# Retention and a GELU feed-forward: three stores on another queue, two loads on another queue, and k ahead of v in one chunk

## The chip, the cores and the metric

The kernel runs on one core of a Trainium2 chip. The metric is the device time of one execution in microseconds (us); the time given is the median of several runs. Five engines work side by side, each with its own instruction stream: TensorE (PE, matrix products), VectorE (DVE), ScalarE (ACT), GpSimd (POOL) and SyncE (SP). SP only issues transfers here; ACT and POOL issue transfers between their other instructions. An instruction that waits holds up everything behind it on its own engine.

## The reference

Four batches, eight heads, a sequence of 768 and a head size of 64. For every head, a decaying state is updated and read at each step:

```
state = gamma[None, :, None, None] * state + einsum('bhd,bhe->bhde', k[:, :, t], v[:, :, t])
y[:, :, t] = scale * einsum('bhd,bhde->bhe', q[:, :, t], state)
```

The result, as 3072 tokens of 512 numbers, goes through a feed-forward of width 2048:

```
h = x @ w_in
g = 0.5 * h * (1.0 + tanh(c * (h + 0.044715 * h * h * h)))
return g @ w_out
```

Inputs and output are 32-bit floats; the kernel multiplies in 16 bits.

## The kernel before

The sequence is cut into six chunks of 128 steps. A chunk has four batches, so (c,b) names the work of chunk c and batch b. For each (c,b) q, k and v are loaded (256 KB each, `load1`, L101 to L105), scaled by the decay and cast to 16 bits (`prep1`, L176 to L194), and for chunks 0 and 1 q and k are transposed on PE (`mm_T`, L235; T(c,b) in this text). From there follow the scores (`mm_A`, L260), masked on DVE (L278), the output y (`mm_yc`, `mm_yi`), and the new state (`mm_s`, `ev_S`). Then comes the feed-forward of the chunk: `moe1` or `moe1_two` (h and GELU, 16 blocks of 128) and `moe2` (the second product), whose result `ev_O` (L458 to L466) copies from PSUM to `o_sb` and stores to memory.

The order of every engine is written out by hand: instructions run on each engine in the order in which the program lists them. `run(units, after)` (L484) goes through a list of pieces of PE work and puts other work after the piece with a given number.

Around the change:

- While PE does the second product of chunk 0, chunk 1 is prepared. `preps(1, b)` (L586) scales q on DVE, scales k on POOL and casts v on ACT. The stores of chunk 0 are issued by POOL, between these k scalings.
- Chunk 1 is loaded by SP (L591 to L599), except v(1,0) and v(1,1), which ACT issues between its GELUs (L577). `hold` (L126) makes the first of SP's loads wait until part of w_out has landed.
- `load(2)` (L615) puts all loads of chunk 2 on SP. q comes in 16 pieces of 64 KB, in a layout that DVE can transpose (`load_blk`, L107); k and v come batch by batch, v first. From chunk 3 on, k is also loaded in 16 such pieces, beside its ordinary load.
- For chunk 2 POOL does all preparation: for each batch it scales q, scales k, casts v (`prep`, L207). PE still transposes k of chunk 2.
- q is kept in two buffers, k and v in six buffers each; `o_sb` has four.

Of the kernel before, what the change touches and what calls it, by code (L numbers as in the profile page):

```python
# [16 lines left out]
def kernel(  # L17
# [9 lines left out]
    nc = tc.nc  # L27
    B, H, S, Dh = q.shape
    C = 128
    NCk = S // C  # L30
# [49 lines left out]
    BLK = {"q": (2, 3, 4, 5), "k": (3, 4, 5)}  # L80
# [12 lines left out]
    def ld_tile(nm, c, b):  # L93
        if nm == "q":
            t = ld_all(("q32", c)).rearrange("p (b hp) a d -> p b (hp a d)", b=B)
            return t[:, b].rearrange("p (h d) -> p h d", h=H)
        if (nm, c, b) not in raw:
            raw[nm, c, b] = ld.tile([128, H, Dh], F32, tag=f"{nm}32", bufs=6, name=f"{nm}32")
        return raw[nm, c, b]

    def load1(eng, nm, c, b):  # L101
        eng.dma_start(  # L102
            out=ld_tile(nm, c, b),
            in_=srcs[nm][b, :, c * C:(c + 1) * C, :].rearrange("h p d -> p h d"),
        )  # L105

    def load_blk(nm, c):  # L107
        t = ld_all((nm + ("32" if nm == "q" else "T32"), c))
        src = srcs[nm].rearrange("b (hp j) s (dd d) -> j dd s (b hp) d", j=2, dd=2)
        for j in range(2):  # L110
            for dd in range(2):
                for a in range(4):
                    p0, t0 = (2 * j + dd) * 32, c * C + a * 32
                    nc.sync.dma_start(  # L114
                        out=t[p0:p0 + 32, :, a, :], in_=src[j, dd, t0:t0 + 32]
                    )

    def load(c):
        for nm in "qk":
            if c in BLK[nm]:  # L120
                load_blk(nm, c)
        for b in range(B):
            for nm in "vk":
                load1(nc.sync, nm, c, b)

    def hold(nm, c, b, until):  # L126
# [19 lines left out]
        out=misc[:, 0:1], in_=zero[:, 0:1], func=AF.Gelu_apprx_tanh, scale=1.0  # L146
# [16 lines left out]
    for j in range(2):  # L163
        for hp in range(NHP):
            nc.vector.tensor_scalar(
                out=mask[:, j, hp],
# [291 lines left out]
    def ev_O(c, b):  # L458
        ps = o_ps[c, b]
        rows = out[b * S + c * C:b * S + (c + 1) * C, :]  # L460
        o_sb = op.tile([128, d_model], F32, tag="o", name="o_sb")
        if b == B - 1 and c > 0:
            nc.vector.tensor_copy(out=o_sb, in_=ps)
        else:
            nc.scalar.copy(out=o_sb, in_=ps)  # L465
        (nc.scalar if c == NCk - 1 else nc.gpsimd).dma_start(out=rows, in_=o_sb)  # L466

    def moe2_last(c, b):

# [20 lines left out]
    VE, AC, PO, SY = nc.vector, nc.scalar, nc.gpsimd, nc.sync  # L490
# [88 lines left out]
    def units2(c, b, n=4, tag="o"):  # L579
        u = [(lambda i=i: moe2(c, b, range(i, i + n), tag)) for i in range(0, NF, n)]  # L580
        last = u[-1]
        u[-1] = lambda: (last(), ev_O(c, b))
        return u
# [10 lines left out]
    load1(SY, "k", 1, 1)  # L594
    load1(SY, "q", 1, 2)
    load1(SY, "k", 1, 2)
    load1(SY, "v", 1, 2)
    for nm in "qkv":
        load1(SY, nm, 1, 3)  # L599
    u = [units2(0, b, tag="ooho"[b]) for b in range(B)]  # L600
    run(
        [u[i % 3][i // 3] for i in range(12)] + u[3],
# [10 lines left out]


    load(2)  # L615
    for b in range(B):
        prep(2, b)
# [9 lines left out]
            4: [(att_AY, 1, (3,), "o", 1, (), VE)],  # L627
            6: [(att_S, 1, 3)],
            8: [(att_T, 2, 0), (load, 3)],
            10: [(att_T, 2, 1)],  # L630
            12: [(att_AY, 1, (), "o", 2, (0, 1), None)],
# [17 lines left out]
    for c in range(2, NCk - 1):  # L649
        n = c + 1  # L650
        after = {
            2: [(prep, n, 0)],
            4: [(prep, n, 1)],
            6: [(prep, n, 2), (att_T, n, 0)],
            8: [(prep, n, 3), (att_T, n, 1)],
            9: [(load, n + 1)] if n + 1 < NCk else [],
            12: [(att_AY, n, (), "att", n, (0, 1), None)],
            13: [(att_T, n, 2)],
            15: [(att_T, n, 3)],
            18: [(att_AY, n, (0, 1), "h", n, (2, 3), VE)],  # L660
            20: [(att_S, n, 0)],
            21: [(att_S, n, 1)],
            25: [(att_AY, n, (2, 3), "h", n, (), AC)],
            27: [(att_S, n, 2)],
            28: [(att_S, n, 3)],
        }
        run(
            [(lambda fc=fc: moe1(c, fc)) for fc in range(NF)]
            + [x for b in range(B) for x in units2(c, b)],
            after,  # L670
        )
    c = NCk - 1
# [36 lines left out]
```

## Time and profile before

| what | value |
|---|---|
| median of 9 runs | 219.75 us (219.18 to 220.63) |
| the profiled execution | 219.52 us |
| its span in the trace | 217.4 us |
| TensorE's granted clock | 1.0 in all of the span |
| transfers | 32.88 MB, mean 151 GB/s |
| POOL's stores, L466 | 20, 256 KB each, median 3.4 us to landing |
| SP's loads of k and of v, 256 KB each | 22 and 20, median 4.6 us to landing |
| SP's loads of q in pieces of 64 KB | 64, median 2.7 us to landing |

The profile is one execution. Its page has the busy time of each engine; the span in 40 slices (5.4 us each) with the busy share in tenths; the transfers by queue; and the costliest groups of instructions, by source line. A row of the timeline has the start, the duration, the engine (SPq and ACTq are the transfers that an engine issues; their duration is that of issuing), the line, the operation, what is written and read, and in brackets the idle time just before it with the engine that ended it. The time to landing runs from the start of the issue until the data has arrived.

### The profile page before, as it was taken

Reading aid. Unit: us, or ns where it says so; the run is one execution under the profiler, and the core shown is the slowest. Engines: PE = TensorE matmul, PEld = TensorE weight load, DVE = VectorE, ACT = ScalarE, POOL = GpSimd, SP = SyncE. Lnnn points to the kernel's source line nnn. Section 1 sums busy time; section 2 is a strip of 40 time slices with the busy share of each in tenths; the row PEclk is TensorE's granted clock in tenths of the full one; section 3 lists DMA queues with packets and bytes.
Section 4 is the critical chain, followed back from the end, with each engine's and each line's share of the span. In section 5 each row is a group of like instructions: output and inputs, shape, how many; then the busy total and the mean of one; then the engine's idle time right before and its main releaser. Section 6 shows DMA issues by size and latency. Waiting matters only on the chain.

```text
span 217.4 us, 3916 instructions
## 1 busy us (share of the span) xinstructions
PE 207.7 (96%) x1544; PEld 113.0 (52%) x1544; DVE 85.5 (39%) x152; ACT 87.3 (40%) x150; POOL 98.9 (46%) x119
## 2 busy tenths in 40 slices
PE   7889999969999999999999999999999999999993
PEld 2447644426877655444555444545444545444462
DVE  3445200198844671333781343691253650100001
ACT  2575563134454333266314165213276223466120
POOL 3699200271449722599613699511399411000000
PEclk9999999999999999999999999999999999999999
DMA  7999999997989778997589986488920011200112
GB/s 173 288 248 207 207 204 239 207 303 138 189 184 204 115 147 175 256 263 124 87 155 226 275 169 95 63 161 197 269 87 3 0 48 62 86 0 0 51 64 81
DMA packets 124225, 32.88 MB, mean 151 GB/s; under 512 B 118064, under 2 KB 122544, under 8 KB 124208
## 3 DMA queue, kind: packets, MB, share of 16 engines
q1 hardware_dynamic: 109632, 20.32, 48.0%
q0 software_dynamic: 5824, 9.44, 17.6%
q10 hardware_dynamic: 8752, 2.88, 5.4%
q8 instruction: 12, 0.20, 0.3%
q14 instruction: 5, 0.04, 0.1%
HBM read 30.53 MB, written 6.29 MB: 169 GB/s over the span
## 4 chain that ended last, share of the span: by engine, by line
PE 85%; SPq 5%; DMA 3%; ACT 2%; POOL 2%; issue 1%; DVE 1%
PE o_ps L445 37%; PE h_ps L412 34%; SPq L114 5%; PE spin_ps L152 4%; DMA k<-in_k_dram 3%; PE a_ps L265 3%; PE y_ps L300 3%; PE s_ps L319 2%; PE y_ps L287 2%; PE qkT_ps L242 1%; POOL k L188 1%; ACT qkT L224 1%; ACT g L427 1%; SPq L102 0%; POOL q L199 0%
## 5 line engine op out<-in xcount | busy, mean ns | idle before, releaser
L445 PE MATMUL o_ps<-w_out,g 128*128 128x512 f16 (+1 forms) x400 | 88.1, 371 | 0.0
L412 PE MATMUL h_ps<-xT,w_in 128*128 128x512 f16 (+2 forms) x488 | 86.6, 334 | 0.5 <-ACT g L427 0.5
L427 ACT ACTIVATE g<-h_ps 128x512 f16<-128x512 f32 (+1 forms) x98 | 57.4, 588 | 50.7 <-PE h_ps L412 50.7
L412 PEld LDWEIGHTS <-w_in 128*128 128x128 f16 x488 | 45.7, 98 | 36.9 <-issue 0.7
L445 PEld LDWEIGHTS <-g 128*128 128x128 f16 x400 | 37.7, 98 | 38.8
L278 DVE TENSOR_TENSOR a_sb<-a_ps,mask 128x512 f16<-128x512 f32 x48 | 30.1, 682 | 19.7 <-PE a_ps L265 19.7
L466 POOL DMA_DIRECT2D out_dram<-o_sb x20 | 11.4, 568 | 49.0 <-ACT o_sb L465 39.4
L188 POOL TENSOR_TENSOR k<-k,cst 128x512 f16<-128x512 f32 x24 | 25.5, 1062 | 15.1 <-DMA k<-in_k_dram 15.1
L465 ACT COPY o_sb<-o_ps 128x512 f32<-128x512 f32 x19 | 11.1, 586 | 47.2 <-PE o_ps L445 42.0
L345 POOL TENSOR_TENSOR stg<-st,cst 128x512 f32<-128x512 f16 x16 | 16.4, 1044 | 12.8 <-DVE st L336 11.7
L336 DVE TENSOR_TENSOR st<-s_ps,stg 64x256 f16<-64x256 f32 x32 | 13.5, 421 | 17.8 <-PE s_ps L319 17.2
L199 POOL TENSOR_TENSOR q<-q,cst 128x512 f16<-128x512 f32 x16 | 16.7, 1042 | 1.9 <-DMA q<-in_q_dram 1.9
L251 DVE STREAM_TRANSPOSE qkT<-q 128x512 f16<-128x512 f16 x16 | 11.2, 699 | 12.1 <-POOL q L199 12.1
L188 DVE TENSOR_TENSOR q<-q,cst 128x512 f16<-128x512 f32 x7 | 7.6, 1090 | 18.5 <-DMA q<-in_q_dram 18.5
L224 ACT CAST xT<-y_ps 128x512 f16<-128x512 f32 x15 | 8.3, 588 | 14.9 <-PE y_ps L300 14.8
L199 POOL TENSOR_TENSOR kT<-kT,cst 128x512 f16<-128x512 f32 x12 | 12.5, 1042 | 0.0
L152 PE MATMUL spin_ps<-zero 128*128 128x512 f16 x32 | 10.6, 477 | 1.2 <-DVE zero L144 1.2
L478 DVE COPY o_sb<-o_ps 128x256 f32<-128x256 f32 x1 | 0.4, 425 | 25.2 <-PE o_ps L445 25.2
L185 POOL CAST v<-v 128x512 f16<-128x512 f32 x16 | 9.6, 601 | 0.0
L226 DVE CAST xT<-y_ps 128x512 f16<-128x512 f32 x9 | 5.9, 686 | 7.8 <-PE y_ps L300 7.8
L251 DVE STREAM_TRANSPOSE qkT<-kT 128x512 f16<-128x512 f16 x12 | 8.3, 689 | 1.8 <-POOL kT L199 1.8
L300 PE MATMUL y_ps<-a_sb,v 128*64 128x128 f16 x192 | 8.6, 223 | 0.2 <-DVE a_sb L278 0.2
(33 smaller groups left out, 93.5 us busy)
## 6 DMA issues: line engine op xcount, KB each, us to landing
k<-in_k_dram SPq DMA_DIRECT2D x22, 256.0 KB, 4.6
v<-in_v_dram SPq DMA_DIRECT2D x20, 256.0 KB, 4.6
out_dram<-o_sb POOLq DMA_DIRECT2D x20, 256.0 KB, 3.4
q<-in_q_dram SPq DMA_DIRECT2D x64, 64.0 KB, 2.7
kT<-in_k_dram SPq DMA_DIRECT2D x48, 64.0 KB, 2.7
w_in<-in_moe_w_in_dram POOLq DMA_DIRECT2D x4, 512.0 KB, 9.3
w_out<-in_moe_w_out_dram POOLq DMA_DIRECT2D x4, 512.0 KB, 14.7
q<-in_q_dram SPq DMA_DIRECT2D x6, 256.0 KB, 5.2
```

Of the source, the lines that this page charges most:

```text
L152: nc.tensor.matmul(out=ps, lhsT=zero[:, 0:128], rhs=zero, start=True, stop=True)
L188: eng.tensor_tensor(out=t, in0=src, in1=cst[:, col:col + H].unsqueeze(2).broadcast_to([128, H, Dh]), op=ALU.mult,)
L199: nc.gpsimd.tensor_tensor(out=t, in0=ld_all((key, c))[:, b * NHP:(b + 1) * NHP].rearrange("p hp a d -> p (hp a) d"), in1=cst[:, col:col + ...
L251: nc.vector.transpose(out=t[:, i].rearrange("p hp t -> p (hp t)"), in_=blk16.pop((nm, c, b)).rearrange("p ha d -> p (ha d)"),)
L278: nc.vector.tensor_tensor(out=s, in0=ps[j], in1=mask[:, j], op=ALU.mult)
L300: nc.tensor.matmul(out=y_ps[j * 64:(j + 1) * 64, hp], lhsT=h16["v", c, b][:, 2 * hp + j], rhs=a_sb[c, b, j][:, hp], start=(c == 0), stop=True,
L336: eng.tensor_tensor(out=st[sl, :, b, sl], in0=s_ps[sl, :, sl], in1=stg[sl, :, b, sl], op=ALU.add,)
L345: nc.gpsimd.tensor_tensor(out=stg[:, :, b], in0=st[:, :, b], in1=cst[:, OG:OG + NHP].unsqueeze(2).broadcast_to([128, NHP, 128]), op=ALU.mult,)
L412: nc.tensor.matmul(out=out, lhsT=w_in_sb[wi][:, kc, wr * 128:(wr + 1) * 128], rhs=xT[c][:, kc, t0:t1], start=(kc == 0), stop=(kc == NHP - ...
L427: nc.scalar.activation(out=out, in_=in_, func=AF.Gelu_apprx_tanh, scale=1.0)
L445: nc.tensor.matmul(out=ps[:, n0:n1], lhsT=g_sb[c, fc // 2][:, fc % 2, b * C:(b + 1) * C], rhs=w_out_sb[fc // (NF // NO)][:, fc % (NF // NO ...
L466: (nc.scalar if c == NCk - 1 else nc.gpsimd).dma_start(out=rows, in_=o_sb)
```

## The change

Three edits. The stores of chunk 0 are issued by SP for batches 0, 1 and 2, and by POOL only for batch 3. v(1,2) and v(1,3) are issued by ACT, behind its last GELU of chunk 0, so that SP issues eight loads of chunk 1 and not ten. And in chunk 2, the only one that `load` fills without a block load of k, the order of each batch's loads is k, v.

```diff
         for b in range(B):
-            for nm in "vk":
+            for nm in "vk" if c in BLK["k"] else "kv":
                 load1(nc.sync, nm, c, b)
...
-        (nc.scalar if c == NCk - 1 else nc.gpsimd).dma_start(out=rows, in_=o_sb)
+        if c == NCk - 1:
+            eng = nc.scalar
+        else:
+            eng = nc.sync if c == 0 and b < B - 1 else nc.gpsimd
+        eng.dma_start(out=rows, in_=o_sb)
...
     load1(SY, "k", 1, 2)
-    load1(SY, "v", 1, 2)
-    for nm in "qkv":
-        load1(SY, nm, 1, 3)
+    load1(SY, "q", 1, 3)
+    load1(SY, "k", 1, 3)
+    load1(AC, "v", 1, 2)
+    load1(AC, "v", 1, 3)
```

On SP the order is now: q and k of chunk 1, the three stores, the 16 pieces of q of chunk 2, then k and v of chunk 2.

## The prediction

> **What bounds the kernel now.** I read the page first: the totals, then the slices.
>
> ```profile
> PE 207.7 (96%) x1544; PEld 113.0 (52%) x1544; DVE 85.5 (39%) x152; ACT 87.3 (40%) x150; POOL 98.9 (46%) x119
> ...
> PE   7889999969999999999999999999999999999993
> ...
> DMA  7999999997989778997589986488920011200112
> ```
>
> TensorE (PE) is busy for 207.7 of 217.4 us, and the granted clock is full in every slice. A change that takes no matmul away can only win PE's holes. After the start they lie in slice 9 (a 6, at 43 to 49 us) and around 65 us; from 73 us to the end nothing is listed as waited for by PE. The DMA engines are nearly full up to 60 us. So next come PE's waits in 33 to 73 us, and the rows of its timeline that carry them ("[2.08 <- ...]" is the idle time before the row and who ended it).
>
> ```profile
> PE qkT_ps L242 <- DVE q L188: 2.1, 1, 2.1
> PE qkT_ps L242 <- POOL k L188: 0.6, 2, 0.4
> ```
> ```profile
> 47.73 0.40 PE L242 MATMUL qkT_ps<-iden,q 128*128 128x128 f16 x4 [2.08 <-DVE q L188]
> ...
> 64.72 0.40 PE L242 MATMUL qkT_ps<-iden,k 128*128 128x128 f16 x4 [0.23 <-POOL k L188]
> ...
> 67.28 0.40 PE L242 MATMUL qkT_ps<-iden,k 128*128 128x128 f16 x4 [0.42 <-POOL k L188]
> ```
>
> The three holes, 2.08 + 0.23 + 0.42 = 2.73 us, are the stake. The first is transpose T(1,1) (chunk 1, batch 1), which waits for q(1,1) scaled on VectorE (DVE). Its row and GpSimd's (POOL's) rows beside it:
>
> ```profile
> 44.14 3.53 DVE L188 TENSOR_TENSOR q<-q,cst 128x512 f16<-128x512 f32 x1
> ```
> ```profile
> 43.04 0.63 POOL L466 DMA_DIRECT2D out_dram<-o_sb  x1 [2.33 <-ACT o_sb L465]
> 43.90 0.56 POOL L466 DMA_DIRECT2D out_dram<-o_sb  x1 [0.23 <-ACT o_sb L465]
> 44.48 1.05 POOL L188 TENSOR_TENSOR k<-k,cst 128x512 f16<-128x512 f32 x1
> 45.46 0.58 POOL L466 DMA_DIRECT2D out_dram<-o_sb  x1
> 46.06 1.05 POOL L188 TENSOR_TENSOR k<-k,cst 128x512 f16<-128x512 f32 x1
> ```
>
> The same q row takes 0.68 or 0.69 at 38.80, 49.39 and 52.40. Here it takes 3.53 and ends at 47.67, 0.56 after POOL's unbroken run from 43.90 to 47.11. I read it as DVE held while POOL works without a gap, then running its 0.69.
>
> The other two holes are chunk 2's k, from the DMA by way of POOL:
>
> ```profile
> 59.60 1.05 POOL L199 TENSOR_TENSOR q<-q,cst 128x512 f16<-128x512 f32 x1 [1.85 <-DMA q<-in_q_dram]
> 63.62 1.04 POOL L188 TENSOR_TENSOR k<-k,cst 128x512 f16<-128x512 f32 x1 [2.97 <-DMA k<-in_k_dram]
> 64.61 0.61 POOL L185 CAST v<-v 128x512 f16<-128x512 f32 x1
> 65.19 1.04 POOL L199 TENSOR_TENSOR q<-q,cst 128x512 f16<-128x512 f32 x1
> 66.19 1.03 POOL L188 TENSOR_TENSOR k<-k,cst 128x512 f16<-128x512 f32 x1
> ```
> ```profile
> 45.61 11.27 SPq L114 DMA_DIRECT2D q<-in_q_dram  x16
> 56.98 0.47 SPq L102 DMA_DIRECT2D v<-in_v_dram  x1
> 57.49 0.94 SPq L102 DMA_DIRECT2D k<-in_k_dram  x1
> ```
>
> v(2,0) is issued at 56.98 and lands 3.2 later, at 60.2; k(2,0) lands 6.1 after its issue, at 63.6. That is 1.8 more than the second load of chunk 3 (4.2) or chunk 4 (4.4).
>
> **Part 1: three stores leave POOL for SyncE (SP).** POOL loses three issues: 0.63 + 0.56 + 0.58 = 1.77 us. More important, k(1,1) no longer stands behind two stores that wait for ScalarE's (ACT's) copies. k(1,1) landed at 42.2 and k(1,2) at 44.0 (issue plus latency), so POOL can scale k(1,1) from 42.3 and be idle when DVE comes to q(1,1) at 44.14; q(1,1) landed at 40.5. DVE then ends at 44.9, before PE reaches T(1,1) at 45.65. Gain 2.08, if POOL is idle at 44.14. If both k scalings stood in the way back to back (2 x 1.05, from 44.1), DVE would end at 46.9 and the gain be 0.8; later k landings (part 2) move POOL's k(1,2) away, so I take 2.08. What is late next is chunk 2's k.
>
> A row of the trace bears on this twice: beside POOL's k rows at 7.71 and 10.42, which grew from 1.04 to 1.31, DVE's q rows (7.43, 10.14) kept 0.69; whoever came second waited. The Trainium skill, "GPSIMD Engine Reference", section "8. Key points", says that GpSimd shares its SBUF interfaces with VectorE, and that instructions with two SBUF inputs contend; the q scaling is one, so these rows agree. By the rule alone, which names no DMA issue, the k scalings still collide and up to 1.3 of the 2.08 would stay; the sum above goes by the rows.
>
> On SP the stores stand behind k(1,3) and ahead of all of chunk 2's loads. The third can't be issued before ACT's copy, 44.33 + 0.58 = 44.91. A 256 KB store from SP isn't in this trace. From below: ACT's own stores, 0.34 to 0.36 an issue. From above: SP's loads issued from 37.8 to 44.3, up to 1.32. So the 16 q pieces start between 45.3 and 48.2 (k(1,3) issued until 44.3, then 3 x 1.3), against 45.61. They took 11.27 for 16; the shortest are 0.49 + 0.05, so 8.6. Their end (now 56.88) moves by d between 45.3 + 8.6 = 53.9 (d = -3.0) and 48.2 + 11.27 = 59.5 (d = +2.6). In the compiled list of instructions and their waits each load reuses one of eight completion counters, and the eighth q piece waits until the third store has landed: issue near 45.7 plus the 5.1 of the store at 45.46 now gives 50.8, against 51.56 now; eight more pieces keep their 0.53 to 0.6. I take d = -0.8.
>
> **Part 2: v(1,2), v(1,3) on ACT.** Two issues leave SP (1.32 + 1.23); the same bytes move through the same, already full DMA engines, so the chunk's last load lands about when it did (50.0). In the compiled list ACT's issue of v(1,2) waits on the counter that q(1,1) used, so ACT stands from 34.12 until about 40.5; behind it stand v(1,0)'s cast and the copies of o_sb. Cover: ACT did nothing between 34.12 and 42.16 but that cast (0.62). Issues cost 0.38 each (as at 27.48 and 29.21) to 1.67 (at 3.03): ACT is free at 40.5 + 0.8 + 0.6 = 41.9, or 44.5 at worst. PE needs the bank of the first o_ps again at 44.61, and its copy takes 0.58: loss between 0 and 0.5. I take 0, the nearer rows. The two v loads share with k(1,1), q(1,2), k(1,2): k(1,2) may land up to 2 x 0.9 (the spacing from 42.2 over 43.1 to 44.0) later than 44.0, at 45.8; with everything 2.08 earlier, T(1,2) is due at 49.0, and POOL's 1.05 still fits.
>
> "DMA: Bandwidth & Descriptors", section "Issuing engines are not separate DMA queues", of the Trainium skill says that another issuing engine saves only sequencer time; no row here shows the move, and by the rule alone part 2 would be worth 0.
>
> **Part 3: k before v in chunk 2.** No instruction is added; k(2,0) takes the first place, which lands at 60.2 + d. POOL scales it right after q(2,0), so one k scaling (1.03) goes from in front of v(2,0)'s landing. Cover for the later v: s and y matmuls need it only after 76 us.
>
> **The sum.** PE without waits would reach T(2,0) at 64.72 - 0.23 - 2.08 = 62.41, and T(2,1) at 67.28 - 2.73 = 64.55. POOL's k(2,0) is ready at 59.6 + d + 1.04 + 1.04 = 61.7 + d: no hole. For k(2,1) it depends on the second load.
> *A. The second load is 1.8 late again.* v(2,0) lands at 63.56 + d; then cast, q, k: T(2,1) at 67.28 - 1.03 + d = 66.25 + d = 65.45, a hole of 0.9. Gain 1.03 - d = 1.83: 219.52 - 1.83 = **217.7**.
> *B. It isn't late.* POOL runs without a gap, k(2,1) is ready at 64.4 + d. Gain 2.73: 216.8.
> After that POOL's chain ends k(2,3) 1.0 + |d| earlier than now, still ahead of T(2,3). From 73 us on PE waits for nothing, and chunk 3's k loads land by about 97.5 against uses up to 105, so the gain is kept.
>
> The profiled execution took 219.52 (span 217.4 and 2.1 around it); the median of the nine is 219.75, 0.23 above, so the median may come out 0.2 higher than the sum.
>
> **Rivals.**
> *C. DMA gives less:* A with d between 0 and +0.8, since stores queue in front of the q pieces. For: full DMA engines up to 50 us. Against: nothing is added to the bytes. Gain 0.2 to 1.0, near 218.8.
> *Nothing:* d near +1.0 in A, the hole merely moves from 47 to 67 us: 219.5. Or the change doesn't do what it says: v(1,2) goes out not behind the GELUs but 6 us later, so part 2 is idle; A and B don't rest on it.
> *Slower:* one mechanism: SP, in order, stands at the three stores, and chunk 2's loads start late. It decides from d = +1.03, q pieces issued until 57.9; at the bound d = +2.6 it costs 1.6: 221.1. For: the third store can't go before 44.91, and SP was never idle there. Against: the store takes the place of a load that SP issued in just that time.
>
> **How the numbers follow.** A 0.45, B 0.25, C 0.12, nothing 0.08, slower 0.10. A measurement of this kernel tells about 0.2% (0.4 us) from no change. Faster is A + B + C = 0.82. The range reaches from B (216.8, less 0.2 for its unknowns) over A and nearly all of C to 219.0.
>
> **What would show it.** Right: DVE's q(1,1) at 0.7; no PE hole near 45.7; the last q piece issued by 56; PE's k hole at T(2,1) 0.9 (A) or none (B). Wrong: q(1,1) still over 1.5; SP's q pieces starting after 47; ACT's first o_sb copy after 43.5; a hole at T(2,0); new holes beyond 73 us.

## The result and the profile after

The changed kernel takes 216.97 us (median of 16 runs, 216.50 to 218.05); the kernel before, on the same chip, takes 219.51 (median of 53). The ratio is 0.9902 with a 95% interval of 0.9883 to 0.9921, so it is about 2.15 us faster (219.51 x 0.0098). The profiled execution took 217.77, with a span of 215.5; it is one of the longer ones.

The page of the changed kernel, the same three rows as before:

```profile
PE 207.4 (96%) x1544; PEld 112.9 (52%) x1544; DVE 82.8 (38%) x152; ACT 87.1 (40%) x150; POOL 96.7 (45%) x116
...
PE   7989999999989999999999999999999999999993
...
DMA  7999999997899787998779976589910012100111
```

PE's busy time is the same within 0.3 us; the 6 of slice 9 has become a 9. What is left of the holes is an 8 in slice 12 (59 to 65 us).

PE's waits of the changed kernel in 33 to 75 us, and the transposes that carried them before, from PE's timeline:

```profile
PE qkT_ps L242 <- POOL k L188: 1.4, 2, 1.0
```
```profile
45.21 0.39 PE L242 MATMUL qkT_ps<-iden,q 128*128 128x128 f16 x4
...
62.79 0.40 PE L242 MATMUL qkT_ps<-iden,k 128*128 128x128 f16 x4 [0.98 <-POOL k L188]
...
65.35 0.40 PE L242 MATMUL qkT_ps<-iden,k 128*128 128x128 f16 x4 [0.42 <-POOL k L188]
```

T(1,1) at 45.21 has no bracket: it waits for nothing. T(2,0) waits 0.98 where it waited 0.23, T(2,1) 0.42 as before.

DVE's row of q(1,1), and POOL's rows around it and in chunk 2:

```profile
43.87 0.68 DVE L188 TENSOR_TENSOR q<-q,cst 128x512 f16<-128x512 f32 x1
```
```profile
41.83 1.04 POOL L188 TENSOR_TENSOR k<-k,cst 128x512 f16<-128x512 f32 x1 [1.22 <-DMA k<-in_k_dram]
45.23 1.04 POOL L188 TENSOR_TENSOR k<-k,cst 128x512 f16<-128x512 f32 x1 [2.36 <-DMA k<-in_k_dram]
...
60.68 1.05 POOL L199 TENSOR_TENSOR q<-q,cst 128x512 f16<-128x512 f32 x1 [5.61 <-DMA v<-in_v_dram]
61.69 1.04 POOL L188 TENSOR_TENSOR k<-k,cst 128x512 f16<-128x512 f32 x1
```

q(1,1) takes 0.68 instead of 3.53. POOL is idle beside it: k(1,1) is done at 42.87 and k(1,2) comes at 45.23. In chunk 2 POOL scales q(2,0) at 60.68, which is 1.08 later than before, and k(2,0), which had landed at 60.84, at once behind it. (The bracket of the q(2,0) row names a load of v, which this row does not read; by the order of the loads it needs the last piece of q last, and that lands at 60.27.)

SP's queue and ACT's rows of the changed kernel:

```profile
41.72 1.60 SPq L102 DMA_DIRECT2D k<-in_k_dram  x1
43.42 3.64 SPq L470 DMA_DIRECT2D out_dram<-o_sb  x3
47.16 9.63 SPq L114 DMA_DIRECT2D q<-in_q_dram  x16
56.84 0.50 SPq L102 DMA_DIRECT2D k<-in_k_dram  x1
57.38 0.59 SPq L102 DMA_DIRECT2D v<-in_v_dram  x1
```
```profile
40.50 1.06 ACTq L102 DMA_DIRECT2D v<-in_v_dram  x2
41.61 0.62 ACT L183 CAST v<-v 128x512 f16<-128x512 f32 x1 [7.76 <-issue]
42.13 1.20 ACT L465 COPY o_sb<-o_ps 128x512 f32<-128x512 f32 x2
```

The three stores one by one (shortest, median and longest issue in ns, then the first and the last start):

```profile
L470 SPq DMA_DIRECT2D out_dram<-o_sb x3: 377/404/2670, 43.4 to 46.7; - x3
```

SP spends 3.64 us on them: 2.67 on the first, from 43.42 on, then 0.38 and 0.40. The first one's copy of `o_sb` had ended at 42.7, so SP did not stand there for its data. The q pieces of chunk 2 therefore start at 47.16 and not at 45.61; they take 9.63 instead of 11.27 and end at 56.79, 0.1 earlier than before. The last piece, issued at 56.27, lands 4.0 later, at 60.27; before, the last one was issued at 56.29 and took 3.1. ACT stands until 40.50, as the waits in the list of instructions said, and its first copy of `o_sb` starts at 42.13.

**Where the time went.** PE's last run of the second product starts at 197.74 instead of 199.68, 1.94 earlier, and nothing behind it has changed. Of this, 0.27 is the start of the program (PE's first long row at 23.10 instead of 23.37, ahead of anything that was changed); the hole at T(1,1) gives 2.25 (2.08 listed, and the modelled overlap of the rows around it); a weight load behind a DVE row gives 0.17; T(2,0) takes back 0.75. The sum, 0.27 + 2.25 + 0.17 - 0.75, is 1.94. The two profiled executions differ by 1.75, the medians by 2.54, and the ratio says 2.15. The profiles cannot account for the difference; the experiments below show one thing that differs between executions, the clock.

### The profile page after: what moved, and what is told of

It reads as the page before. It is cut to its first block, busy times and chain, and to the rows that moved or that the text cites. A ratio compares the mean times of both kernels' runs of the same rounds, so it can differ in the third digit from the quotient of the medians.

```text
span 215.5 us, 3912 instructions
## 1 busy us (share of the span) xinstructions
PE 207.4 (96%) x1544; PEld 112.9 (52%) x1544; DVE 82.8 (38%) x152; ACT 87.1 (40%) x150; POOL 96.7 (45%) x116
## 2 busy tenths in 40 slices
DMA packets 124417, 32.88 MB, mean 153 GB/s; under 512 B 118064, under 2 KB 122544, under 8 KB 124400
## 4 chain that ended last, share of the span: by engine, by line
PE 84%; SPq 5%; DMA 3%; POOL 2%; ACT 2%; issue 1%; DVE 1%; ACTq 0%; DVEq 0%
PE o_ps L445 38%; PE h_ps L412 34%; SPq L114 4%; PE a_ps L265 3%; PE y_ps L300 3%; PE s_ps L319 2%; DMA iden<-rr_ident 2%; PE y_ps L287 2%; PE qkT_ps L242 2%; DMA v<-in_v_dram 2%; PE spin_ps L152 1%; POOL q L199 1%; POOL k L188 1%; ACT qkT L224 1%; ACT g L427 1%
## 5 line engine op out<-in xcount | busy, mean ns | idle before, releaser
L412 PEld LDWEIGHTS <-w_in 128*128 128x128 f16 x488 | 45.7, 98 | 37.0 <-issue 0.7
L188 POOL TENSOR_TENSOR k<-k,cst 128x512 f16<-128x512 f32 x24 | 24.9, 1038 | 16.7 <-DMA k<-in_k_dram 16.7
L470 POOL DMA_DIRECT2D out_dram<-o_sb x17 | 9.7, 568 | 46.5 <-ACT o_sb L465 36.8
L188 DVE TENSOR_TENSOR q<-q,cst 128x512 f16<-128x512 f32 x7 | 4.8, 685 | 18.3 <-DMA q<-in_q_dram 18.3
L183 ACT CAST v<-v 128x512 f16<-128x512 f32 x8 | 5.0, 621 | 10.7 <-issue 7.8
```

The costliest lines, as they stand in the source:

```text
L188: eng.tensor_tensor(out=t, in0=src, in1=cst[:, col:col + H].unsqueeze(2).broadcast_to([128, H, Dh]), op=ALU.mult,)
L412: nc.tensor.matmul(out=out, lhsT=w_in_sb[wi][:, kc, wr * 128:(wr + 1) * 128], rhs=xT[c][:, kc, t0:t1], start=(kc == 0), stop=(kc == NHP - ...
```

## The experiments

Twelve kernels were run. Each expectation names its theories; H is the prediction's, that POOL's unbroken run beside q(1,1) makes the first hole and its order cures it. H2 is what the first four runs made of H; the expectation under "Parts 2 and 3" spells it out. The runs in one table ("holes" are from the one profiled execution; "outside" is the median of time minus span; "low clock" counts executions whose mean granted clock was 0.992 or less; there were none between that and 0.995; two executions of before above 222 us, at 0.981, are not counted):

| kernel | median us | ratio to before (95%) | hole T(1,1) | holes chunk 2 | median span | outside | low clock |
|---|---|---|---|---|---|---|---|
| before | 219.5 to 219.8 | 1 | 2.08 | 0.65 | 217.5 to 217.8 | 2.1 | 38 of 72 |
| changed | 216.97 | 0.9902 (0.9883 to 0.9921) | 0 | 1.40 | 214.7 | 2.27 | 0 of 17 |
| part 1 alone | 218.39 | 0.9960 (0.9935 to 0.9986) | 0 | 1.57 | 216.1 | 2.26 | 0 of 12 |
| part 2 alone | 217.23 | 0.9911 (0.9881 to 0.9941) | 0.23 | 0.59 | 215.4 | 1.80 | 2 of 12 |
| part 3 alone | 218.72 | 0.9984 (0.9954 to 1.0014) | 2.09 | 0 | 216.6 | 2.09 | 4 of 12 |
| parts 1, 2 | 217.93 | 0.9936 (0.9911 to 0.9961) | 0 | 1.15 | 215.6 | 2.26 | 0 of 12 |
| parts 1, 3 | 218.36 | 0.9937 (0.9914 to 0.9960) | 0 | 1.51 | 216.0 | 2.30 | 0 of 6 |
| parts 2, 3 | 216.79 | 0.9863 (0.9839 to 0.9888) | 0 | 0.42 | 215.0 | 1.79 | 1 of 6 |
| stores last on SP | 217.33 | 0.9897 (0.9871 to 0.9923) | 0 | 0 | 214.9 | 2.42 | 0 of 6 |
| two idle products | 217.67 (one run) | | 0 | 0.42 | 215.6 | 2.07 | 0 of 1 |
| POOL reordered | 217.85 | 0.9922 (0.9898 to 0.9946) | 0 | 1.76 | 215.8 | 2.10 | 0 of 11 |
| POOL reordered, 2, 3 | 217.39 | 0.9901 (0.9862 to 0.9939) | 0 | 0.26 | 215.6 | 1.75 | 0 of 6 |
| hole filled | 219.03 | 0.9981 (0.9953 to 1.0010) | 0.15 | 0 | 217.1 | 2.03 | 0 of 12 |
| issues and products mixed | 217.95 | 0.9937 (0.9911 to 0.9962) | 0.56 | 0.42 | 216.1 | 1.90 | 0 of 12 |

Two cautions for reading it. The rows were measured in several batches, each beside the kernel before, so rows are compared by their ratios before their medians. And executions of one kernel at full clock lie about 1 to 2 us apart, with the profiled one at either end: the changed kernel's (217.77) is among its longest, those of the last two rows are the shortest of theirs. So the holes tell what became of a wait, but they do not rank kernels whose medians are 1 us apart.

### Part 1 alone

```diff
-        (nc.scalar if c == NCk - 1 else nc.gpsimd).dma_start(out=rows, in_=o_sb)
+        if c == NCk - 1:
+            eng = nc.scalar
+        else:
+            eng = nc.sync if c == 0 and b < B - 1 else nc.gpsimd
+        eng.dma_start(out=rows, in_=o_sb)
```

> Only part 1: the three stores of chunk 0 go through SP; the rest is the kernel before. Theory H (PE's holes): the hole at T(1,1), 2.1 us, comes from the stores on POOL and is gone, DVE's q(1,1) takes 0.7; but SP issues ten loads and three stores ahead of q of chunk 2, whose pieces start 1 to 2 us later than in the changed kernel (49 rather than 47.2), and the holes at T(2,0) and T(2,1) grow to about 2 in all. Gain 0.3 to 1.3 us: 218.2 to 219.2. Rival R1 (the two loads taken off SP bring the gain): 219.5, no change. Rival R2 (the order of k and v brings it): 219.5.

Measured: 218.39, ratio 0.9960. DVE's row of q(1,1) and POOL's row beside it:

```profile
44.34 1.16 DVE L188 TENSOR_TENSOR q<-q,cst 128x512 f16<-128x512 f32 x1
```
```profile
43.91 1.04 POOL L188 TENSOR_TENSOR k<-k,cst 128x512 f16<-128x512 f32 x1 [0.78 <-DMA k<-in_k_dram]
```

POOL's product k(1,2) began first, at 43.91, and ends at 44.95; DVE's row ends at 45.50, 0.55 later. DVE waited for the product in hand and no longer, and T(1,1) has no hole. In its place T(2,0) waits 1.15 and T(2,1) 0.42, with v(2,0) still loaded first. So part 1 takes away the first hole by itself, and part of the gain is given back 17 us later: the holes of chunk 2 grow from 0.65 to 1.57.

### Part 2 alone

```diff
-    load1(SY, "v", 1, 2)
-    for nm in "qkv":
-        load1(SY, nm, 1, 3)
+    load1(SY, "q", 1, 3)
+    load1(SY, "k", 1, 3)
+    load1(AC, "v", 1, 2)
+    load1(AC, "v", 1, 3)
```

> Only part 2: v(1,2) and v(1,3) on ACT; the rest is the kernel before. Theory H: the stores stay on POOL, so DVE's q(1,1) stays at about 3.5 us and the hole at T(1,1) at about 2: 219.5 within 0.5. It may shift if k(1,2) lands later and leaves POOL a gap. Rival R1: this part alone brings most of the gain, 217.3 to 218.

Measured: 217.23, ratio 0.9911. H missed by 2.3 us; part 2 alone brings nearly all of the gain, with the stores still on POOL. POOL's and DVE's rows, then ACT's and SP's:

```profile
43.57 1.19 POOL L466 DMA_DIRECT2D out_dram<-o_sb  x2 [2.97 <-ACT o_sb L465]
44.76 1.06 POOL L188 TENSOR_TENSOR k<-k,cst 128x512 f16<-128x512 f32 x1
```
```profile
43.92 0.68 DVE L188 TENSOR_TENSOR q<-q,cst 128x512 f16<-128x512 f32 x1
```
```profile
40.52 1.60 ACTq L102 DMA_DIRECT2D v<-in_v_dram  x2
...
42.69 1.07 ACT L465 COPY o_sb<-o_ps 128x512 f32<-128x512 f32 x2
```
```profile
43.29 12.77 SPq L114 DMA_DIRECT2D q<-in_q_dram  x16
```

ACT, held until 40.52 and busy with its two issues until 42.12, copies `o_sb` later, so POOL's stores come out at 43.57 instead of 43.04, and k(1,1), behind them, at 44.76: after q(1,1), which ran in its usual 0.68 while POOL did nothing but issue transfers. The prediction asked of this standing only what it costs ACT. SP, with two loads less, starts chunk 2's q pieces 2.3 us earlier (43.29 against 45.61), and q(2,0) is scaled at 58.59, 1.0 earlier; chunk 2's holes stay at 0.59 although PE reaches T(2,0) 2.2 us sooner. The hole at T(1,1) is 0.23.

### Part 3 alone

```diff
-            for nm in "vk":
+            for nm in "vk" if c in BLK["k"] else "kv":
```

> Only part 3: k ahead of v in chunk 2; the rest is the kernel before. Theory H: the hole at T(1,1) stays at 2.1, the holes at T(2,0) and T(2,1), 0.65 in all, shrink or go: gain 0 to 0.6, 218.9 to 219.5. Rival R2: gain 1.5 to 2, 217.5 to 218.

Measured: 218.72, ratio 0.9984, which is not told from no change. The 2.09 at T(1,1) stays (q(1,1) takes 3.54) and both holes of chunk 2 are gone. The profiled execution, at 219.84, is one of four with a low clock. First two rows of PE's timeline, then PE, PEld, DVE, ACT, POOL, granted clock (the eighth number), DMA share and GB/s for each microsecond from 47 to 53:

```profile
47.71 0.40 PE L242 MATMUL qkT_ps<-iden,q 128*128 128x128 f16 x4 [2.09 <-DVE q L188]
...
48.17 1.75 PE L445 MATMUL o_ps<-w_out,g 128*128 128x512 f16 x4
```
```profile
47.00:48.00 1.00, 0.29 (x5) 0.29 (x6) 1.00 (x2) 0.00 (x0) 0.10 (x1) 1.00 1.11 326
48.00:49.00 1.00, 1.00 (x9) 0.56 (x7) 1.00 (x3) 0.00 (x0) 0.35 (x1) 0.66 1.18 339
49.00:50.00 1.00, 1.00 (x6) 0.45 (x5) 1.00 (x2) 0.00 (x0) 0.69 (x1) 0.50 1.10 238
50.00:51.00 1.00, 1.00 (x16) 0.61 (x15) 0.32 (x2) 0.00 (x0) 0.00 (x0) 0.50 0.89 138
51.00:52.00 1.00, 1.00 (x11) 0.45 (x9) 1.00 (x2) 0.50 (x2) 0.00 (x0) 0.63 0.78 129
52.00:53.00 1.00, 1.00 (x14) 0.76 (x13) 0.20 (x1) 0.60 (x2) 0.00 (x0) 1.00 0.16 19
```

The clock goes from 1.00 to 0.50 about 0.6 us after the hole has ended and is back before 52 (at about 48.3 and 51.7, worked out from the means of the slices): four matmuls of 128x512 take 1.75 instead of 1.03. In full-speed time the four slices from 48 to 52 lose 0.34 + 0.50 + 0.50 + 0.37 = 1.7 us. The four executions with a low clock have a median of 219.8, the eight others 218.39. So in such an execution the first hole costs more than its 2.08. The kernel before shows the same two groups: 38 executions with a mean clock of 0.992 or less, median 219.85, and 34 at 0.998 or more, median 218.99. The profiled execution of before, from which the prediction was made, is one of the 34.

### Parts 1 and 2 without 3

```diff
-            for nm in "vk" if c in BLK["k"] else "kv":
+            for nm in "vk":
```

> Parts 1 and 2 without part 3 (v stays ahead of k in chunk 2). Theory H: as the changed kernel, T(1,1) without a hole; k(2,0) comes one load later, about 0.9 us, but q(2,0) of POOL was the later one there, so the holes at T(2,0), T(2,1) sum to 1.4 to 2.3: gain 1.2 to 2.1, 217.4 to 218.3. Rival R2: without the order of k and v little is left, 219 to 219.5.

Measured: 217.93, as expected. q(1,1) takes 0.68 at 44.23, and now POOL's product, k(1,2) at 44.52, is the one that comes second and takes 1.28. SP issues the stores from 42.85 in 2.67 and starts the q pieces at 45.63; q(2,0) is scaled at 58.59, but k(2,0) only at 61.79, because v(2,0) was first: holes of 0.73 and 0.42. Part 3, on top of 1 and 2, is worth 217.93 - 216.97 = 1.0 in the medians and 0.75 by the ratios, whose intervals overlap a little. The two traces do not show this gain: the holes are 1.15 here and 1.40 in the changed kernel, because there q(2,0) was scaled 2.1 later (60.68), and k(2,0) came at 61.69, hardly earlier than the 61.79 here.

### Parts 2 and 3, stores still on POOL

```diff
-            eng = nc.sync if c == 0 and b < B - 1 else nc.gpsimd
+            eng = nc.gpsimd
```

> Parts 2 and 3 without part 1: the stores of chunk 0 stay on POOL. After the single parts, theory H2: the hole at T(1,1) is DVE's q(1,1) meeting POOL's k scalings, and part 2 alone cures it because ACT, held by its two issues, copies o_sb later and so POOL's stores and k(1,1) come later than q(1,1); what is left is set by when SP gets to chunk 2's q pieces (43.3 with part 2 alone, 47.2 in the changed kernel, since part 1 puts three stores in front). H2: q pieces from 43.3, k(2,0) lands first, no hole over 0.2 at T(2,0), at most 0.3 at T(2,1): 216.4 to 216.9, no slower than the changed kernel's 216.97. Rival H (part 1 is what cures T(1,1)): hole of 2 back, 218.5 to 219.5.

Measured: 216.79, ratio 0.9863; the interval touches that of the changed kernel. Without part 1 the kernel is not slower: by its span, 215.0 against 214.7, it does a little less, by its time a little more, since the time outside the span is 1.79 instead of 2.27. q(1,1) ran from 44.54 in 0.68 while POOL was busy with issues (43.90 to 45.10). One of six executions had a low clock (219.61). Part 1 isn't needed as long as q(1,1) comes before k(1,1) on POOL.

### Parts 1 and 3 without 2

```diff
-    load1(SY, "q", 1, 3)
-    load1(SY, "k", 1, 3)
-    load1(AC, "v", 1, 2)
-    load1(AC, "v", 1, 3)
+    load1(SY, "v", 1, 2)
+    for nm in "qkv":
+        load1(SY, nm, 1, 3)
```

> Parts 1 and 3 without part 2: v(1,2), v(1,3) stay on SP. H2: T(1,1) has no hole (no store on POOL); SP's q pieces start at 47.5 as with part 1 alone; with k first, q(2,0) on POOL is the late one (61.3 there), k(2,0) done 2.1 later at 63.4: the holes stay as with part 1 alone less 0 to 0.2: 218.0 to 218.4. Rival (the order of k and v is worth a load, 0.9): 217.4 to 217.7.

Measured: 218.36, ratio 0.9937, as H2 expected. Here q(2,0) is the late one: POOL scales it at 61.30 and k(2,0) right behind it, at 62.31. SP's rows:

```profile
45.36 1.87 SPq L470 DMA_DIRECT2D out_dram<-o_sb  x3
47.33 10.45 SPq L114 DMA_DIRECT2D q<-in_q_dram  x16
57.82 0.49 SPq L102 DMA_DIRECT2D k<-in_k_dram  x1
```

With all ten loads of chunk 1 ahead of the stores, the issue of the q pieces ends at 57.78, 1.0 later than in the changed kernel, and k ahead of v brings nothing that can be told apart from part 1 alone (218.36 and 218.39; the intervals of the ratios overlap widely). Part 2 on top of 1 and 3 is worth 218.36 - 216.97 = 1.4 in the medians and 0.8 by the ratios, whose intervals overlap a little. That it does so by making room on SP for the three stores fits the 1.0, but the traced holes differ by only 0.11 (1.51 and 1.40), so it is not shown.

### The stores behind all of chunk 2's loads

Against the changed kernel; the three stores stay on SP, but as its last work before chunk 3:

```diff
+        if c == 0 and b < B - 1:
+            late.append((rows, o_sb))
+            return
+        (nc.scalar if c == NCk - 1 else nc.gpsimd).dma_start(out=rows, in_=o_sb)
...
     load(2)
+    for rows, o_sb in late:
+        SY.dma_start(out=rows, in_=o_sb)
```

> The changed kernel, but the three stores of chunk 0 are issued by SP behind all loads of chunk 2, not ahead of them. H2: q pieces start at 43.3, q(2,0) of POOL at about 57.5, no holes at T(2,0) and T(2,1) (0.98 + 0.42, and 0.34 of overlap with them): 1.2 to 1.7 less than the changed kernel: 215.3 to 215.8. Rival (the DMA engines set the pace, not SP's order): the pieces take as long to land, 216.5 to 217.

Measured: 217.33, ratio 0.9897: missed. The q pieces start at 42.94, q(2,0) is scaled at 57.82, and T(2,0) and T(2,1) wait for nothing. PE's last run starts at 196.26, 1.5 earlier than in the changed kernel's profile. What PE gained does not reach the total: the profiled span is 1.0 shorter (214.5), the median span 0.2 longer (214.9 against 214.7), and 2.42 us lie outside it. The changed kernel's profiled execution is one of its longest, so part of the 1.5 may be that; where the rest goes wasn't found.

### Two idle products on POOL

Against the changed kernel; the added products write a tile that nothing reads:

```diff
         prep1(PO, "k", c, b)
+        if (c, b) == (1, 1):
+            o = o_kept[0, 1]
+            for _ in range(2):
+                PO.tensor_tensor(
+                    out=junk.rearrange("p (h d) -> p h d", h=H),
+                    in0=o.rearrange("p (h d) -> p h d", h=H),
+                    in1=cst[:, OQ:OQ + H].unsqueeze(2).broadcast_to([128, H, Dh]),
+                    op=ALU.mult,
+                )
```

> The changed kernel, with two extra products on POOL (o_sb of batch 1 times a constant into a scratch tile, results unused) right behind k(1,1), so that POOL runs from about 43.3 to 45.4 while DVE comes to q(1,1) at 43.9. If DVE waits until POOL has a gap: q(1,1) takes 2.2 to 3.3 us (the k(1,2) scaling follows at 45.2 to 46.5), a hole of 0.5 to 2 at T(1,1). If DVE waits only for the product in hand: about 1.2. If POOL doesn't hold DVE: 0.7 and no hole.

One run, 217.67. DVE's and POOL's rows:

```profile
44.30 1.13 DVE L189 TENSOR_TENSOR q<-q,cst 128x512 f16<-128x512 f32 x1
```
```profile
43.83 2.49 POOL L599 TENSOR_TENSOR junk<-o_sb,cst 128x512 f32<-128x512 f32 x2 [0.68 <-ACT o_sb L467]
```

Two products back to back do not hold DVE for both: its row ends at 45.43, 0.56 after the first product would end undisturbed (43.83 + 1.04 = 44.87), the same distance as in part 1 alone, and POOL's pair takes 2.49 instead of 2.08. Here the engines took turns product by product, in one execution. This speaks against the prediction's reading that DVE is held "while POOL works without a gap".

### POOL's stores behind its k scalings

Against the kernel before; the same three stores, still on POOL, after the four k of chunk 1:

```diff
+        if c == 0 and b < B - 1:
+            late.append((rows, o_sb))
+            return
...
         prep1(AC, "v", c, b)
+        while c == 1 and b == 3 and late:
+            rows, o_sb = late.pop(0)
+            PO.dma_start(out=rows, in_=o_sb)
```

> The kernel before with one thing moved: POOL issues the stores of batches 0, 1, 2 of chunk 0 behind the four k scalings of chunk 1, not between them. SP, ACT and the order of k and v are as before. Theory H2 (DVE's q(1,1) is kept waiting by POOL's run of k scalings and store issues): q(1,1) takes 0.7 to 1.2, no hole over 0.5 at T(1,1), no execution with a mean clock of 0.992 or less; chunk 2's holes grow to about 1.1, as with parts 1 and 2: 217.4 to 218.0. Rival (it is the load taken off SP, or the hold on ACT, that helps): 219 or more.

Measured: 217.85, ratio 0.9922, as H2 expected. Nothing has moved to another engine, SP's order is untouched, and:

```profile
43.76 0.68 DVE L188 TENSOR_TENSOR q<-q,cst 128x512 f16<-128x512 f32 x1
```
```profile
43.95 1.40 POOL L188 TENSOR_TENSOR k<-k,cst 128x512 f16<-128x512 f32 x1 [0.76 <-DMA k<-in_k_dram]
```

DVE came first and kept 0.68; POOL's product, 0.2 behind it, took 1.40. The hole at T(1,1) and the low clock are gone (0 of 11). This shows the cause of the first hole: the order of stores and k scalings on POOL.

### The same with parts 2 and 3

The diff is the last one, with the diffs of parts 2 and 3.

> The stores on POOL behind the k scalings, with parts 2 and 3 of the change. H2: no hole at T(1,1) in any execution, SP free for chunk 2's q pieces from 43.3, k first: holes at T(2,0) and T(2,1) 0.5 or less in all: 216.0 to 216.6, the fastest of all. Rival (the stores' bytes, now at 49 to 52, delay the q pieces as much as SP's issue of them did): 216.8 to 217.3.

Measured: 217.39, ratio 0.9901: missed. The profiled execution (216.57, span 214.8) has one hole of 0.26 left, as expected; the other five lie 0.2 to 1.3 us above it, and their traces were not taken. It is no better than the changed kernel.

### The first hole filled with idle matmuls

Against the kernel before; nine matmuls of zeros into a bank that nothing reads, between the pieces of PE's work before T(1,1):

```diff
-            12: [(att_T, 1, 1), (preps, 1, 2)],
+            12: [(spin, 9), (att_T, 1, 1), (preps, 1, 2)],
```

> The kernel before with nine products of zeros (1.9 us, into a scratch bank, unused) on PE in front of T(1,1), so that PE is busy in most of the 2.1 us hole. Executions of the kernel before fall in two groups: mean clock 1.0 (median 218.6) and 0.988 to 0.992 (median 219.8). If the hole makes the granted clock drop (theory K): nearly all at 0.998 or more, median 218.2 to 218.9, faster than before though PE does more. Rival (the drop comes from elsewhere, or the products add time): the groups stay, 219.3 to 220.

Measured: 219.03, ratio 0.9981, not told from no change. PE's rows:

```profile
45.29 2.10 PE L152 MATMUL spin_ps<-zero 128*128 128x512 f16 x9
47.55 0.40 PE L242 MATMUL qkT_ps<-iden,q 128*128 128x128 f16 x4 [0.15 <-DVE q L188]
```

T(1,1) comes no earlier (47.55, in an execution that runs 0.2 ahead already at q(1,1)) and q(1,1) still takes 3.54, but none of 12 executions had a low clock, against 38 of 72. So it is PE's idling that brings the clock down. In time, two groups remain all the same (218.3 to 218.8 and 219.2 to 220.4), at full clock: part of the spread of this kernel has another cause, which stays open, and what the low clock costs in the median is not shown by this run.

### Issues and products mixed

Against the changed kernel; on POOL, behind k(1,1), a small transfer, an idle product, a transfer, an idle product, to rebuild the run that stood beside q(1,1):

```diff
+        if (c, b) == (1, 1):
+            o = o_kept[0, 1]
+            for i in range(2):
+                PO.dma_start(out=junk[:, 64 * i:64 * i + 64], in_=o[:, 64 * i:64 * i + 64])
+                PO.tensor_tensor(
...
+                )
```

> The changed kernel with extra work on POOL behind k(1,1): transfer issue, product, transfer issue, product, on o_sb of batch 1 and into scratch tiles, unused. It copies the pattern that POOL had in the kernel before. If a product queued behind a transfer issue keeps DVE out (theory M): q(1,1) takes 2.5 to 4, a hole of 1 to 2.5 at T(1,1), and, by theory K, a mean clock of 0.992 or less in some of the executions: median 217.6 to 219.5. If DVE waits only for the product in hand, as with the two products alone (1.13): 1.0 to 1.9, hole below 0.8, 216.9 to 217.5.

Measured: 217.95, ratio 0.9937. POOL's and DVE's rows:

```profile
43.72 0.62 POOL L600 DMA_DIRECT2D junk<-o_sb  x1 [0.59 <-ACT o_sb L468]
44.36 1.06 POOL L601 TENSOR_TENSOR junk<-o_sb,cst 128x512 f32<-128x512 f32 x1
45.34 0.59 POOL L600 DMA_DIRECT2D junk<-o_sb  x1
45.95 1.05 POOL L601 TENSOR_TENSOR junk<-o_sb,cst 128x512 f32<-128x512 f32 x1
```
```profile
43.96 2.01 DVE L190 TENSOR_TENSOR q<-q,cst 128x512 f16<-128x512 f32 x1
```

DVE's row began during the first issue, was overtaken by the product behind it, and ended at 45.97, 0.55 after that product's end (45.42) and beside the second issue: it was held by one product, not by the whole run. In the kernel before the row ended 0.56 after the second product of a run of the same form. So neither theory is confirmed to the number. A product directly behind an issue can go ahead of a DVE row that began 0.3 to 0.4 earlier (here, and in before: 44.14 against 44.48); why DVE got its turn after one product here and after two there stays open.

## Why the prediction was right, and where it was off

**The main step holds.** The first hole was DVE's q(1,1) held by POOL's order, and the changed kernel has neither. The reordering on POOL alone shows the cause, since nothing else moved. Expected for the total was 217.7, measured 216.97; expected for the gain 1.83, measured 2.15. That the profiled execution (217.77) lies beside the 217.7 is partly luck: it has holes of 1.40 left where case A has 0.9, and an earlier start (0.27) and two small gains that no term had (0.17 each) made up for that.

**The mechanism of the hold was read too simply.** DVE is not held by POOL's activity: beside transfers alone it ran in 0.68 (part 2 alone; parts 2 and 3). It waits for a product, usually for one (1.13 and 1.16 instead of 0.68); why it was held for two in the kernel before stays open. The result was the same, because the changed kernel has no product beside q(1,1).

**"I take d = -0.8" was off.** The step was that SP issues three stores in place of two loads within its bounds, and that the eighth q piece would be free by 50.8. d came out at -0.1. The first store alone took 2.67 to issue, more than the upper bound of 1.32 that was taken from SP's loads, so the third went out at 46.7 and not at 45.7, and the eighth q piece at 51.8. The q pieces began at 47.16, later than the 47 that the prediction named as a sign against it, and the last went out at 56.27, not by 56. They ran faster in between (9.63). The first store's copy had ended at 42.7 and does not explain the 2.67; why SP stood wasn't settled.

**"No hole" at T(2,0) was wrong.** The sum had k(2,0) ready at 61.7 + d. With d = -0.1 and the last q piece landing 4.0 after its issue instead of 3.1, q(2,0) starts at 60.68, and T(2,0) waits 0.98: the hole that was named as a sign against. At T(2,1) the wait is 0.42, between case A's 0.9 and case B's none: v(2,0) landed 4.4 after its issue, not late, which is B's condition. POOL then runs without a gap, as B said, but k(2,1) is ready at 65.29, 1 us later than B's 64.4 + d. So a total near A's came out of B's condition with a later q(2,0), in the profiled execution. The median execution has a span 0.8 shorter than the profiled one; it wasn't traced, and whether T(2,0) waits less in it is open.

**"I take 0" for part 2 was wrong.** Its loss was rightly bounded: ACT was free of both issues and the cast at 42.2, against the 41.9 expected, and its first copy started at 42.13. Its gain was not looked for. Alone it brings 0.9%, by two ways that the prediction had in hand: the delayed copies push POOL's stores and k(1,1) behind q(1,1), and SP reaches chunk 2's q pieces 2.3 us earlier. With parts 1 and 3 in place it is worth 0.8 by the ratios and 1.4 in the medians. "DMA: Bandwidth & Descriptors" of the Trainium skill, section "Issuing engines are not separate DMA queues", by which a move to another issuing engine saves sequencer time alone, agrees as far as bytes go (32.88 MB in both kernels), and here the time that SP was free earlier is one of the two ways; the other, the delay on ACT, is no saving.

**Part 3's price of 1.03 is met in the number, not shown in its mechanism**: on top of parts 1 and 2 it is worth 1.0 in the medians and 0.75 by the ratios, but the two traces have k(2,0) on POOL at nearly the same time. Alone it takes away both chunk 2 holes (0.65), and beside the full-clock executions of before in its own batch (218.70) its own (218.39) are 0.3 faster.

**A term was missing: the clock.** In 38 of 72 executions of before the mean clock was low, with about 0.9 us between the medians of the two groups (219.85 and 218.99); in the changed kernel in none of 17. The profile of before showed "9" in every slice of the clock and could not tell. As an estimate, its weight is 38/72 x 0.86 = 0.45 us of the mean gain, about the size of the 0.3 that the forecast was short. That it is what the forecast lacked is not shown: the profiled execution of before, at full clock, was itself 0.5 above its group's median, and the kernel with the filled hole has both groups of times without any low clock.

**The slower rival** did not come about, but its mechanism did: SP stood at the stores and the q pieces began 1.55 late. The issue of the 16 pieces made it up, but the last of them landed 0.9 later than before, at 60.27, which is most of T(2,0)'s hole.

## What to carry to other kernels

When two engines take turns, look at who starts first: an instruction that is held can be cured by reordering the other engine's queue, and a delay of that engine can do it too, as part 2 did by accident. A load or store moved between queues is worth what it frees on the queue that it leaves, so follow the next late transfer there before calling the move free. A hole on TensorE of some 2 us can cost more than its length, and one profile at full clock does not show it: look at the granted clock of all executions.

## What the runs showed of the hardware

- **The clock fell after a short hole.** PE idle for 2.1 us was followed by a granted clock of 0.50 for about 3.4 us (48.3 to 51.7) in the traced execution of part 3 alone; the mean clock was low (0.992 or less) in 4 of its 12 executions and in 38 of 72 of before. In the kernels whose traced hole is 0.6 or less, and in the one with the hole filled by idle matmuls, none shows it except 3 of 18 of the two kernels that have part 2 and the stores at their old place on POOL (none of these three was traced). "TensorE: Matmul & The Clock Gate" of the Trainium skill, section "Part 1: The HAM clock gate (the "warmup" mystery)", says that the rate is full or half and is set by free-running windows of about 3.4 us, half after an idle one. The 0.50 agrees; a hole shorter than one such window was enough here, in some executions and not in others.
- **DVE and POOL take turns.** Of two 128x512 products, the one that started second waited: POOL's grew from 1.04 to 1.28 and 1.40, DVE's from 0.68 to 1.13 and 1.16. Where issues and products alternate on POOL, a product behind an issue also overtook a DVE row that had begun 0.34 to 0.40 earlier, and DVE's row took 2.01 and 3.54. POOL's transfer issues alone did not lengthen DVE's 0.68.
- **Time outside the span differs by kernel**: 1.8 with v on ACT and stores on POOL, 2.1 before (1.72 to 2.32), 2.26 to 2.30 with stores on SP (but 1.90 and 2.07 when idle work on POOL is added), 2.42 with stores last on SP. It decides between kernels that are 0.3 us apart; its cause was not looked for.
